# Seven block products for the first group of a channel mixer, and wider additions of key chunks

## The chip, the cores and the metric

One core of a Trainium2 chip. The metric is the time of one execution on the device in microseconds (us), lower is better; of several runs the median is given.

## The reference

Attention with capped scores (4 batches, 12 heads, 448 positions, head size 64), then a mixer over its output: a token product with a residual, and a channel product with a residual. All of it is in fp32.

```python
def _attn_ref(q, k, v, cap):
    scores = cap * np.tanh(scale * np.matmul(q, k.transpose(0, 1, 3, 2)) / cap)
    attn = np.exp(scores - np.max(scores, axis=-1, keepdims=True))
    attn = attn / (np.sum(attn, axis=-1, keepdims=True) + 1e-09)
    return np.matmul(attn, v)
...
def _moe_ref(x, w_tok1, w_tok2, w_ch1, w_ch2):       # x: (4, 448, 768)
    h = np.maximum(x.transpose(0, 2, 1) @ w_tok1, 0.0) @ w_tok2
    u = x + h.transpose(0, 2, 1)
    h2 = np.maximum(u @ w_ch1, 0.0) @ w_ch2          # 768 -> 1536 -> 768
    return u + h2
```

## The kernel before

**Precision.** Most products are made with three matmuls on two rounded parts of each operand: high x high, low x high, high x low (`TERMS`). So every operand of such a product needs a high part, a copy on ScalarE, and a low part, a subtraction of that copy on VectorE. The channel weights come as 64-bit numbers and are decoded in chunks of 512 columns (`decode`, lines 232 to 314): `first` on ScalarE, `second` and `third` on VectorE, then high and low parts. Two work tiles (`wz`) and two raw tiles (`wraw`) carry the chunks.

**Stages.** First the attention: for each pair of heads and each chunk of 128 keys (the last chunk, of 64 keys, is packed for two pairs of heads) TensorE makes scores (L424, L429, L435), ScalarE takes tanh and exp (L454, L462), TensorE multiplies by v (L502, L505). VectorE adds the exponentials over the key chunks in `acc` (`add_two` L524, `add_third` L531, `add_packed` L541: two instructions of 64x448 for each pair of heads), and TensorE sums `acc` over partitions (`add_rows`, L553). Beside it, in pieces, runs the token mixing of batches whose attention is done: transposes (L632), `tok1` (L660), `tok2` (L683).

Then the channel product, in 6 groups of 256 hidden columns. For a batch and a group, `ch1` makes 256 hidden columns from 768 (36 matmuls, L1033) and `ch2` adds their product with the second weights to `u`.

- In groups 1 to 5 the second product is done for two batches at once, `ch2_pair`: the hidden blocks of two batches and the weights are combined so that seven block products (p1 to p7) do the work of eight. That is 63 matmuls (7 products, 3 column blocks `mc`, 3 terms; L992) for 72. The operands are differences of hidden blocks, formed on GpSimd (`form`, L929), and each gets its high and low part (`split`, L953 and L958). Six operand tiles (`NO`) take them. Products run in two chains, a and b. A chain keeps adding to its PSUM banks, and after each product VectorE adds the banks to `u`: the first two banks of chain a by one wide instruction (L1020), the others singly (L1080). The chain's next product in the same bank waits for that addition (L984). The weights need seven blocks per chunk in place of four: `blocks` (L276, four sums on VectorE) and two high and two low parts (L289, L290, L298, L299).
- In group 0 it is done by batch, `ch2`: 36 matmuls (L1070), six additions (L1080), with high and low parts of all 256 hidden columns (L1048, L1051).

**The order.** The whole program's order is made when it is built. A planner (`Plan`, lines 106 to 185) holds a list of jobs for each engine, with an estimated cost, the estimated times of what they need, and a slack; among the jobs that are ready it takes the one with the lowest ready time plus slack. `plan.pe` is TensorE's planned time. `fill()` is called between matmul groups, and lays in up to 2500 ns of token mixing (`background`, `chunk`); where TensorE has to wait in the plan (`await_key`, `await_time`) it also takes such pieces, as long as there are any. `Ring`s count the buffers. Each engine then runs its own list in that order.

`first_group` (L1111) orders group 0: `ch1` of a batch if its split u is ready (at most two ahead of `ch2`), else a `ch2`, else a piece of token mixing. Batch 3 can be split only when all token mixing has ended, since its parts lie over the token weights (L1117 to L1120). The last `ch2` of the group comes after the first `ch1` of group 1. `open_m1` (L884) makes room for the operand tiles as soon as the attention has ended. The last pair of the kernel, (5, 1), has its own order of products (`FINISH`) and some low parts on GpSimd (`RELIEF`).

## Time and profile before

| | |
|---|---|
| median of 3 runs | 571.34 us (571.0 to 572.15) |
| the profiled execution | 571.16 us, of it span 569.4 us |
| granted TensorE clock | 0.998 |
| attention, with token mixing beside it | to about 194 us of the span |
| group 0, with the rest of the token mixing | about 189 to 294 us |
| groups 1 to 5 | about 294 to 569 us |

Times in the rows are microseconds of the span, unless marked ns. PE is TensorE's matmuls, PEld its weight loads, DVE VectorE, ACT ScalarE, POOL GpSimd; L12 is line 12 of the kernel. "a <- b" in brackets tells the idle time before an instruction and what ended it. The busy time of matmuls overlaps (367 ns each, though they start about every 204 ns), so the loads' starts are the better clock of TensorE.

### The profile page before, as it was taken

Reading aid. Unit: us, or ns where it says so; the run is one execution under the profiler, and the core shown is the slowest. Engines: PE = TensorE matmul, PEld = TensorE weight load, DVE = VectorE, ACT = ScalarE, POOL = GpSimd, SP = SyncE. Lnnn points to the kernel's source line nnn. Section 1 sums busy time; section 2 is a strip of 40 time slices with the busy share of each in tenths; the row PEclk is TensorE's granted clock in tenths of the full one; section 3 lists DMA queues with packets and bytes.
Section 4 is the critical chain, followed back from the end, with each engine's and each line's share of the span. In section 5 each row is a group of like instructions: output and inputs, shape, how many; then the busy total and the mean of one; then the engine's idle time right before and its main releaser. Section 6 shows DMA issues by size and latency. Waiting matters only on the chain.

```text
span 569.4 us, 8201 instructions
## 1 busy us (share of the span) xinstructions
PE 561.8 (99%) x3012; PEld 431.8 (76%) x3012; DVE 491.4 (86%) x857; ACT 298.9 (52%) x415; POOL 61.0 (11%) x66
## 2 busy tenths in 40 slices
PE   8999999999999999999999999999999999999996
PEld 2333455544646799999999899999999999998995
DVE  2999999998999998637859899988999899959597
ACT  7999999899899443222234433334342424224230
POOL 0000100000000000000004202020202030303050
PEclk9999999999999999999999999999999999999999
DMA  7554767666451232000212223112220212010055
GB/s 244 174 157 117 236 193 230 208 205 203 112 167 34 70 108 75 0 2 0 75 38 74 75 55 93 37 39 74 75 69 7 83 66 75 0 39 0 3 195 193
DMA packets 26780, 55.50 MB, mean 97 GB/s; under 512 B 7024, under 2 KB 16752, under 8 KB 26736
## 3 DMA queue, kind: packets, MB, share of 16 engines
q1 hardware_dynamic: 24144, 48.21, 26.7%
q0 software_dynamic: 2160, 6.39, 3.9%
q8 instruction: 24, 0.39, 0.3%
q10 hardware_dynamic: 432, 0.34, 0.2%
q14 instruction: 20, 0.16, 0.1%
HBM read 47.97 MB, written 5.59 MB: 94 GB/s over the span
## 4 chain that ended last, share of the span: by engine, by line
PE 85%; DVE 7%; ACT 3%; DMA 3%; issue 1%; SPq 0%; DVEq 0%; ACTq 0%
PE ps_g L1033 28%; PE ps_o L992 21%; PE ps_pv L502 7%; PE ps_qk L424 6%; PE ps_h L660 6%; PE ps_u L683 5%; PE ps_o L1070 5%; PE ps_t L632 2%; PE ps_s L553 2%; PE ps_qk L435 1%; PE ps_pv L505 1%; ACT e L454 1%; DMA wraw<-in_w 1%; DVE ops L958 1%; ACT e L462 1%
## 5 line engine op out<-in xcount | busy, mean ns | idle before, releaser
L1033 PE MATMUL ps_g<-uhl,wc 128*128 128x448 f32 x648 | 137.3, 367 | 0.0
L992 PE MATMUL ps_o<-ops,wc 128*128 128x448 f32 x630 | 131.0, 367 | 0.8 <-ACT hid L914 0.5
L1033 PEld LDWEIGHTS ps_g<-uhl,wc 128*128 128x128 f32 x648 | 120.9, 188 | 11.2 <-issue 0.7
L992 PEld LDWEIGHTS ps_o<-ops,wc 128*128 128x128 f32 x630 | 117.5, 188 | 13.0 <-issue 1.3
L1080 DVE TENSOR_TENSOR u<-u,ps_o 128x448 f32<-128x448 f32 (+1 forms) x163 | 92.3, 612 | 11.0 <-PE ps_o L1070 10.6
L953 ACT ACTIVATE ops<-hid 128x448 fp32r<-128x448 f32 x70 | 38.8, 574 | 116.4 <-POOL hid L929 70.3
L454 ACT ACTIVATE e<-ps_qk,tsc 128x896 f32<-128x896 f32 x84 | 81.6, 1037 | 7.9 <-PE ps_qk L424 4.0
L929 POOL TENSOR_TENSOR hid<-hid 128x448 f32<-128x448 f32 x40 | 48.5, 1212 | 345.9 <-ACT hid L914 287.3
L462 ACT ACTIVATE e<-e,near 128x896 f32<-128x896 f32 x84 | 85.5, 1077 | 0.1
L502 PE MATMUL ps_pv<-e,vn 128*64 128x448 f32 x288 | 60.5, 549 | 0.9 <-ACT e L462 0.9
L1020 DVE TENSOR_TENSOR u<-u,ps_o 128x896 f32<-128x896 f32 x36 | 38.9, 1081 | 16.9 <-PE ps_o L992 16.9
L958 DVE TENSOR_TENSOR ops<-hid,ops 128x448 fp32r<-128x448 f32 x67 | 45.4, 694 | 1.4 <-ACT ops L953 1.4
L1033 PE MATMUL ps_g<-last_u,wc 128*128 128x448 f32 x216 | 45.3, 367 | 0.0
L502 PEld LDWEIGHTS ps_pv<-e,vn 128*64 128x64 f32 x288 | 18.0, 136 | 34.7 <-issue 24.8
L1033 PEld LDWEIGHTS ps_g<-last_u,wc 128*128 128x128 f32 x216 | 40.6, 188 | 3.8
L255 ACT ACTIVATE wz<-wraw 128x512 f32<-128x512 f32 x36 | 23.8, 672 | 28.1 <-DVE wc L310 11.3
L660 PE MATMUL ps_h<-wc,last_u 128*128 128x384 f32 x176 | 33.3, 337 | 0.0
L683 PE MATMUL ps_u<-last_u,wc 128*128 128x448 f32 x144 | 32.8, 371 | 0.0
L660 PEld LDWEIGHTS ps_h<-wc,last_u 128*128 128x128 f32 x176 | 30.8, 188 | 1.8 <-issue 1.3
L683 PEld LDWEIGHTS ps_u<-last_u,wc 128*128 128x128 f32 x144 | 26.4, 188 | 6.0 <-issue 1.8
L1070 PE MATMUL ps_o<-ops,wc 128*128 128x448 f32 x144 | 30.9, 367 | 0.0
L541 DVE TENSOR_TENSOR acc<-acc,e 64x448 f32<-64x448 f32 x48 | 29.7, 619 | 1.3
(75 smaller groups left out, 632.7 us busy)
## 6 DMA issues: line engine op xcount, KB each, us to landing
wraw<-in_wc SPq DMA_DIRECT2D x36, 512.0 KB, 3.5
qkraw<-in_qk SPq DMA_DIRECT2D x23, 448.0 KB, 4.0
vn<-in_v SPq DMA_DIRECT2D x24, 224.0 KB, 3.3
rb<-rs SPq DMA_DIRECT2D x48, 112.0 KB, 3.3
out_t<-u SPq DMA_DIRECT2D x23, 224.0 KB, 2.0
qkhi<-in_qk POOLq DMA_DIRECT2D x12, 416.0 KB, 4.3
qkhi<-qkraw POOLq DMA_DIRECT2D x3, 416.0 KB, 3.9
wraw<-in_w SPq DMA_DIRECT2D x2, 512.0 KB, 6.0
```

Source lines behind the costliest of these rows:

```text
L454: nc.scalar.activation(e, ps[:, :, :S], AF.Tanh, scale=tsc)
L462: nc.scalar.activation(e, e, AF.Exp, scale=near)
L502: nc.tensor.matmul(o, vn[x % 3][:, j * NF + c], es[b, p, c][:, j], start=first, stop=last)
L660: nc.tensor.matmul(ps[:, :HALF], w, x, start=(n == 0), stop=(n == len(mm) - 1))
L683: nc.tensor.matmul(ps[:, :S], h1[:, hi, t, cs], w2s[:, wi, t, :], start=(n == 0), stop=(n == 3 * NT - 1))
L929: job(FORM, *cost, lambda: e.tensor_tensor(h[:, out], h[:, a], h[:, b], op=ALU.subtract), *deps, slack=500.0, key=("f", n, key))
L958: e.tensor_tensor(t[:, 1], src, t[:, 0], op=ALU.subtract)
L992: nc.tensor.matmul(ps[:, :S], wblock[mc][wi][:, a], x[:, xi], start=first and m == 0, stop=m == 2, skip_group_check=not first,)
L1020: nc.vector.tensor_tensor(u[b][:, cc:cc + 2], u[b][:, cc:cc + 2], ps[:, :, :S], op=ALU.add)
L1033: nc.tensor.matmul(ps[:, i, :S], w[:, wi, cc, fs], uhl[b][:, ui, cc, :], start=(n == 0), stop=(n == 3 * NC - 1))
L1070: nc.tensor.matmul(ps[:, :S], w[:, wi, i, cs], x[:, gi, i, :], start=(n == 0), stop=(n == 3 * GF - 1))
L1080: nc.vector.tensor_tensor(u[b][:, cc, r], u[b][:, cc, r], ps[:, r], op=ALU.add)
```

## The change

Group 0's second product is done by pairs, with seven products. Its weights are decoded with the seven blocks. The tile of group 0's second weights has room for the blocks of the first chunk and one more part, so those of the second and third chunk go into three of the six operand tiles, which group 0 doesn't use then: it has three for itself (`NI`, ring `oi`), and group 1's operands wait until group 0's second product is done. The two chunks in spare tiles wait for `m1`, the pool of the operand tiles. The chunk's sums take a tile of the attention's pool (`wi`, one buffer) until the later pool is open. The first pair is placed behind `ch1` of batch 1, the second behind the first `ch1` of group 1. Pair (0, 0) takes its products in the order `EARLY`: p1, p2, p7, p6, p4, p5, p3, and its chain b takes the other PSUM buffer of ring `a` for its first two banks, so that ring `c` stays with the token mixing. The splits of group 0 have a more urgent slack (`HASTE`).

The packed key chunks of two pairs of heads are added by one job with two instructions of 64x896 in place of two jobs with two of 64x448 each, once both pairs' sums exist.

In the last pair the low part of p3 goes to GpSimd too.

```diff
+NI = 3
+HASTE = -300.0
+EARLY = tuple(PRODUCTS[n] for n in (0, 5, 1, 2, 3, 4, 6))
-RELIEF = {(NG - 1, 1): ("p2", "p7", "p4")}
+RELIEF = {(NG - 1, 1): ("p2", "p7", "p4", "p3")}
...
+    def spot():
+        return "ws" if ("m2",) in done else "wi"
...
-                job("dve", 4 * 190, 4 * 190 + 70, blocks, (*key, 3), ("m2",), room("ws"), slack=slack, key=(*key, 5))
+                job("dve", 4 * 190, 4 * 190 + 70, blocks, (*key, 3), *([room("ws"), ("m2",)] if key[1] else [lambda: rings[spot()].room()]),
+                    slack=slack, key=(*key, 5))
...
-            s = held["s"] = late["m2"].tile([P, NS, P], F32, tag="ws", name="ws", bufs=2)
-            held["ws"] = rings["ws"].take(1)
+            at = spot()
+            s = held["s"] = (px if at == "wi" else late["m2"]).tile([P, NS, P], F32, tag=at, name=at, bufs=rings[at].n)
+            held["ws"] = rings[at].take(1)
...
+    def blocks_of(g, mc):
+        if g or mc == 0:
+            return wblock[mc]
+        spare = late["o"][:, NI:].rearrange("p n x s -> p n (x s)").rearrange("p n (k c) -> p n k c", c=P)
+        return (spare[:, 0], spare[:, 1]) if mc == 1 else (wend[0], spare[:, 2])
...
-                slack, since + mc * DU * st, after[1], wblock[mc] if combine else None,
+                slack, since + mc * DU * st, after[1] if g or mc == 0 else [("m1",)],
+                (lambda: blocks_of(g, mc)) if combine else None,
...
-        holds["e", b, p, c] = rings["e"].take(3 if c == NF else 2)
+        holds["e", b, p, c] = rings["e"].take(2)
...
             if i:
-                add_packed(b, p)
+                add_packed(b, p - 1)
...
-                keys = [(n, b, p - k) for n in ("third", "packed") for k in range(2)]
+                keys = [("third", b, p - 1), ("third", b, p), ("packed", b, p - 1)]
...
-        elif c == NF:
-            add_packed(b, p)
...
     def add_packed(b, p):
-        q, i = divmod(p, 2)
-
         def add():
-            for j in range(2):
-                r = half(i, j)
-                t = accs[b, q][0][r, i, j]
-                nc.vector.tensor_tensor(t, t, es[b, p - i, NF][r, i], op=ALU.add)
-            holds["e", b, p - i, NF].read(done["packed", b, p])
-
-        job("dve", 1272, 1260, add, ("add", b, p), ("exp", b, p - i, NF), slack=2500.0, key=("packed", b, p))
+            acc = accs[b, p // 2][0].rearrange("p i j s -> p (i j) s")
+            e = es[b, p, NF]
+            for r, t in ((slice(0, D), acc[:D, 0::3]), (slice(D, P), acc[D:, 1:3])):
+                nc.vector.tensor_tensor(t, t, e[r], op=ALU.add)
+            holds["e", b, p, NF].read(done["packed", b, p])
+
+        job("dve", 2030, 2150, add, ("add", b, p), ("add", b, p + 1), ("exp", b, p, NF), slack=2500.0, key=("packed", b, p))
...
-    w0, w0_steps = group_weights(0, slack=20000.0, since=65000.0, stagger=STAGGER)
+    w0, w0_steps = group_weights(0, combine=True, slack=WEIGHTS, since=SINCE, stagger=STAGGER)
...
+        done["m1",] = plan.pe
...
-        source = {"h0": ("r", n, 0), "h1": ("r", n, 0) if n[0] == NG - 1 else ("f", n, "t4"), "h3": ("f", n, "t2")}
+        source = {"h0": ("r", n, 0), "h1": ("r", n, 0) if n == (0, 0) or n[0] == NG - 1 else ("f", n, "t4"), "h3": ("f", n, "t2")}
...
-            deps = [source.get(of, ("f", n, of)), room("o")] + ([("sh", n, before)] if before else [])
+            deps = [source.get(of, ("f", n, of)), room("o" if n[0] else "oi")]
+            deps += [("sh", n, before)] if before else []
+            deps += [("ch2", 0)] if n[0] == 1 else []
...
-        return FINISH if n[0] == NG - 1 else PRODUCTS
+        return FINISH if n[0] == NG - 1 else EARLY if n == (0, 0) else PRODUCTS
...
-        job("act", 468, 568, high, *deps, slack=800.0, key=("sh", n, k))
+        job("act", 468, 568, high, *deps, slack=800.0 if n[0] else HASTE, key=("sh", n, k))
...
-            if mc == len(have):
+            if mc == len(have) and n == (0, 0):
+                tag = "a" if chain == "b" and mc == 0 else "b"
+                await_time(rings[tag].room)
+                if tag == "a":
+                    other = ps_a.tile([P, 2, 512], F32, tag="a", name="ps_o3")
+                    have += [other[:, 0], other[:, 1]]
+                    holds_of["b"] += [rings["a"].take(6)] * 2
+                else:
+                    have.append(ps_b.tile([P, 512], F32, tag="b", name="ps_o"))
+                    holds_of[chain].append(rings["b"].take(4 if chain == "a" else 3))
+            elif mc == len(have):
...
     def first_group(w):
-        started, g, at = 2, [], []
-        while len(g) < B:
+        started, n, pair = 2, 0, False
+        while n < B:
...
-            n, m = len(g), len(at)
-            t = plan.ready([("split", n, 0)]) if n < started and n - m < 2 else None
+            if n == 2 and not pair:
+                t = plan.ready([("s", (0, 0), PRODUCTS[0][0]), ("wc2", 0, 0)])
+            else:
+                t = plan.ready([("split", n, 0)]) if n < started else None
             if t is not None and t <= plan.pe + PATIENCE:
-                g.append(ch1(w[0], n))
-            elif m < n and (t := plan.ready([("g", 0, m)])) is not None and t <= plan.pe + PATIENCE:
-                ch2(w[1], m, g[m], False)
-                at.append(plan.pe)
+                if n == 2 and not pair:
+                    ch2_pair((0, 0), False)
+                    pair = True
+                else:
+                    ch1(w[0], n, 0, n // 2)
+                    n += 1
             elif not chunk():
                 rest()
             fill()
-        for m in range(len(at), B - 1):
-            ch2(w[1], m, g[m], False)
-        return w[1], B - 1, g[-1], False, 0
...
-            if g == 1 and b == 0:
-                ch2(*pend)
-                done["ch2", 0] = plan.pe
...
-            if b % 2:
+            if b % 2 or (g == 1 and b == 0):
                 if before is not None:
                     ch2_pair(before, False)
                     if before[1] == 1:
                         done["ch2", before[0]] = plan.pe
-                before = g, b // 2
+                before = (g, b // 2) if b % 2 else None
```

## Rows read from the trace of the kernel before

**Rows 1.** The page's first part: busy us, share of the span, instructions.

```profile
PE 561.8 (99%) x3012; PEld 431.8 (76%) x3012; DVE 491.4 (86%) x857; ACT 298.9 (52%) x415; POOL 61.0 (11%) x66
```

**Rows 2.** Weight loads' waits, 60 to 190 us: total us, times, longest.

```profile
PEld ps_pv L502 <- issue: 19.5, 76, 0.7
PEld ps_u L683 <- DVE acc L541: 0.7, 1, 0.7
```

**Rows 3.** Weight loads in order of time: start us, us, line, count.

```profile
194.43 0.16 PEld L553 LDWEIGHTS ps_s<-acc,ones 128*32 128x32 f32 x8 [0.31 <-ACT uhl L781]
...
221.91 2.33 PEld L1070 LDWEIGHTS ps_o<-ops,wc 128*128 128x128 f32 x12
...
259.81 12.25 PEld L1070 LDWEIGHTS ps_o<-ops,wc 128*128 128x128 f32 x60
...
344.74 12.87 PEld L992 LDWEIGHTS ps_o<-ops,wc 128*128 128x128 f32 x63
```

**Rows 4.** Order of time at the first pair of group 1.

```profile
317.25 2.92 PE L992 MATMUL ps_o<-ops,wc 128*128 128x448 f32 x13 [0.49 <-ACT hid L914]
...
318.77 1.09 DVE L1020 TENSOR_TENSOR u<-u,ps_o 128x896 f32<-128x896 f32 x1 [1.99 <-PE ps_o L992]
```

**Rows 5.** By stretch: busy us of PE, loads, VectorE, ScalarE, GpSimd; clock; DMA.

```profile
205.00:294.20 89.20, 89.20 (x464) 82.71 (x464) 60.27 (x112) 25.68 (x44) 0.00 (x0) 1.00 0.14 45
320.00:500.00 180.00, 180.00 (x882) 164.91 (x881) 168.11 (x303) 64.63 (x108) 33.14 (x28) 1.00 0.17 53
```

**Rows 6.** VectorE's groups: count, busy us, mean ns, idle before.

```profile
L1080 DVE TENSOR_TENSOR u<-u,ps_o 128x448 f32<-128x448 f32 x161 | 91.7, 615 | 11.0 <-PE ps_o L1070 10.6 <-PE ps_o L992 0.4
L1020 DVE TENSOR_TENSOR u<-u,ps_o 128x896 f32<-128x896 f32 x36 | 38.9, 1081 | 16.9 <-PE ps_o L992 16.9
L958 DVE TENSOR_TENSOR ops<-hid,ops 128x448 fp32r<-128x448 f32 x67 | 45.4, 694 | 1.4 <-ACT ops L953 1.4
L282 DVE TENSOR_TENSOR wz<-wz 128x128 f32<-128x128 f32 x15 | 4.4, 293 | 0.5
```

**Rows 7.** Group 0's weights, low parts: ns min/median/max, first and last start.

```profile
L310 DVE TENSOR_TENSOR wc<-wz,wc x6: 676/686/693, 115.9 to 210.5; 128x512 fp32r<-128x512 f32 x6
```

**Rows 8.** GpSimd's differences: ns min/median/max, first and last start.

```profile
L929 POOL TENSOR_TENSOR hid<-hid x40: 1142/1157/1537, 303.0 to 552.8; 128x448 f32<-128x448 f32 x40
```

**Rows 9.** Order of time at 303 us, GpSimd and VectorE.

```profile
303.00 4.39 POOL L929 TENSOR_TENSOR hid<-hid 128x448 f32<-128x448 f32 x3 [146.71 <-ACT hid L914]
...
303.47 1.35 DVE L310 TENSOR_TENSOR wc<-wz,wc 128x512 fp32r<-128x512 f32 x1 [0.22 <-ACT wc L306]
...
304.74 1.64 DVE L298 TENSOR_TENSOR wc<-wz,wc 128x512 fp32r<-128x512 f32 x1
...
306.31 1.51 DVE L299 TENSOR_TENSOR wc<-ws,wc 128x384 fp32r<-128x384 f32 x1
```

**Rows 10.** Weight loads of the token mixing, 221.3 to 260 us.

```profile
L683 PEld LDWEIGHTS ps_u<-last_u,wc 128*128 128x128 f32 x54 | 10.1, 188 | 0.8
L660 PEld LDWEIGHTS ps_h<-wc,last_u 128*128 128x128 f32 x45 | 8.0, 188 | 0.1
L632 PEld LDWEIGHTS ps_t<-ident,u 128*128 128x128 f32 x24 | 2.9, 140 | 0.3
```

**Rows 11.** High part of an operand on ScalarE, group.

```profile
L781 ACT ACTIVATE uhl<-u 128x448 fp32r<-128x448 f32 x18 | 9.7, 595 | 13.0 <-DVE u L689 13.0
```

**Rows 12.** Order of time in the tail: last pairs on TensorE, end of VectorE.

```profile
538.62 26.43 PE L992 MATMUL ps_o<-ops,wc 128*128 128x448 f32 x126
...
557.51 0.61 DVE L958 TENSOR_TENSOR ops<-hid,ops 128x448 fp32r<-128x448 f32 x1
...
559.05 7.18 DVE L1080 TENSOR_TENSOR u<-u,ps_o 128x448 f32<-128x448 f32 x14
```

**Rows 13.** Additions of key chunks: two of 64x448 in time, 128x896 as group.

```profile
191.19 1.25 DVE L541 TENSOR_TENSOR acc<-acc,e 64x448 f32<-64x448 f32 x2
...
L524 DVE TENSOR_TENSOR acc<-e 128x896 f32<-128x896 f32 x24 | 25.9, 1078 | 4.9 <-ACT e L462 4.8
```

More of the change, by code (lines that the diff above doesn't have):

```diff
@@ L949, in high @@
         def high():
[L950 to L952 removed]
+            ring = rings["o" if n[0] else "oi"]
+            t = late["o"][:, len(ring.holds) % ring.n]
+            operand[n, k] = t, ring.take(1)
             nc.scalar.activation(t[:, 0], src, AF.Copy)
```

24 lines of the change are left out of this document (13 added, 11 removed).

## The prediction

> **What bounds the kernel now.** I read the page's first part, then who waited for whom, then TensorE's weight loads in order of time, because the busy time of overlapping matmuls says little by itself. TensorE is busy 99% of the span, VectorE 86% [rows 1]. In the attention the loads' idle times never exceed 0.7 us apiece, and the same 0.7 stands where nothing was waited for at all ("issue"); the rows that name VectorE are single ones of that size, of which one is shown [rows 2]. So VectorE does not hold TensorE up there. Behind the attention the loads run end to end: 60 of the old channel product took 12.25 us, 0.204 us each, and a pair of 63 took 12.87 us [rows 3], also 0.204. One wait stands out in mid-kernel: the first pair of the second group began at 317 us after 0.49 us of idle matmul [rows 4]. From the attention's end on the kernel is bound by TensorE, so a matmul taken out there is worth 0.204 us, less what TensorE then waits.
>
> VectorE has room in the first group and little later: 60.3 of 89.2 us (68%) from 205 to 294 us, 168.1 of 180 us (93%) in the steady stretch, where TensorE still keeps the pace of rows 3 [rows 5].
>
> **The change, part by part.**
>
> *Matmuls.* Four batches of 36 become two pairs of 63: 144 less 126 is 18, at 0.204 us: **-3.67 us**, all of it in the bound engine.
>
> *VectorE and GpSimd in the first group.* Out go 24 additions of 0.615 us (14.8 us) and four low parts of 896 columns (4.3 us at the wide addition's price). In come, for a pair, four wide additions of 1.081 and thirteen of 0.615 us, so 24.6 us for two pairs, and 14 low parts of 448 columns, 8.6 us at 0.615 each (their mean, 0.694, has blocked ones in it) [rows 6]. Each of three weight chunks gains four block sums of 0.292 us [rows 6] and a second, narrower low part of at most the 0.686 us of the first [rows 7]: 1.7 to 1.9 us, three times, 5.4 us. The sum is +19.5 us: 60.3 becomes 79.8 us in a stretch that shrinks to about 85.5, or 93%. That is the steady stretch's share, so by itself it costs TensorE nothing. ScalarE has 25.7 us of work there [rows 5]; fourteen high parts of 0.60 us (the price of rows 11) add 8, which it can take. GpSimd gets eight differences of 1.157 us, the median [rows 8], in time that it now spends idle.
>
> Those eight are not free for VectorE. Where three of them ran at 303 us, in 4.39 us, three VectorE subtractions of two SBUF tiles beside them took 1.35, 1.64 and 1.51 us [rows 9] in place of 0.69 and less: some 0.8 us more each. Over the whole kernel it is far less: 67 low parts at 0.694 against 0.615 us lose 5.3 us to 40 differences, 0.13 us each [rows 6, 8]. The ends are 8 x 0.13 = 1 us and 8 x 0.8 = 6.4 us of VectorE; I take the lower, since it averages the same pattern, and the upper makes a rival. The Trainium skill ("SBUF — State Buffer", "Who interferes with whom") says that a VectorE instruction with two SBUF inputs and a GpSimd instruction that reads SBUF shut each other out for a whole instruction; the trace at 303 us agrees, and were all eight to block so, the sum would come out near 573 us instead.
>
> *What covers the waits.* From 221 us, where the old product begins, to 259.8 us, where its last 60 matmuls run unbroken [rows 3], TensorE also has 22 us of token mixing: 54 and 45 matmuls and 24 transposes [rows 10]. Those 60 matmuls then hide the splits of the last batch. After the change the token pieces must lie between the products of one pair of 63. By the code it offers 17 places with up to 2.5 us each, but chains of transpose, product and eviction keep the pieces from coming faster than they do now. So I expect the token work to end near the pair's end, and one of two bills comes. If it ends earlier, the last two products of the new order, p5 and p3, meet in the same bank: the wide addition starts 0.30 us after its sixth matmul's slot (317.25 plus 6 x 0.204, to 318.77 us) [rows 4] and takes 1.08 us, three matmuls cover 0.61 us, so TensorE waits **0.8 us**; and the third batch's first product takes the bank pair just used, **0.8 us** again. If it ends later, splitting the last batch starts only after the third batch's product: 0.60 us on ScalarE [rows 11], 0.62 on VectorE and two handovers, 1.3 to 1.5 us uncovered. I take **+1.6 us**; bounds 0 (pieces left for every wait) and 3.5 (a loaded VectorE doubles each wait).
>
> *Weights.* The last of the six low parts of group 0's weights starts at 210.5 us [rows 7], about 11 us before the pair. The second-product chunks now take their sums in one spare tile, so the three follow each other. Two also wait for their place in the spare operands, free once the attention's last row sums ran at 194.4 us [rows 3]; that is over before they need it. Queued behind a waiting chunk are only the next one and, by the two work tiles, the second group's first ones. I cost it at nothing: token pieces fill a start that is late by some us. If that cover is gone, 2 us.
>
> *Second pair, first pair of group 1.* The second pair has three operand tiles, so four of its seven splits fall inside its own 12.87 us. 12.3 us of additions and 2.5 of splits make 14.8 us of busy VectorE; back to back such instructions start 0.51 us apart, 14 in 7.18 us [rows 12], which makes it about 13. It just fits. What it pushes back is the second group's weights, and these stand before the pair that already waits at 317 us. I take **+0.3 us**, between -0.5 (that wait gone) and +3.
>
> *Attention.* Two additions of 64x448 take 1.25 us together; twelve times, four of them (2.5 us) give way to two of 64x896, 2.15 us at the price of 128x896 [rows 13]: 4 to 5 us less of VectorE. As rows 2 show no wait of TensorE that this would shorten, I cost it at **0**; the order of pieces shifts, so -1.2 to +0.7.
>
> *Tail.* The split at 557.5 us leaves VectorE, which from there runs without a break to 566.2 us, while TensorE ends at 565.05 us [rows 12]. The end comes forward by at most that 0.61 us and not past the eviction of TensorE's own last matmul: **-0.3 us**, between 0 and -0.5. GpSimd has until the last product for it, some 5 us.
>
> **Sum.** The profiled execution took 571.16 us: 569.4 us of span and 1.76 us around it; it stands 0.18 us below the median of the runs, 571.34. 571.16 - 3.67 + 1.6 + 0.3 - 0.3 = 569.1 us; the median would be 569.3. Between them: **569.2 us**.
>
> **Rivals.**
> - *All of it arrives.* Token pieces stay for every wait in the first pair, and group 1 starts as now: 571.2 - 3.7 - 0.3 + 0.3 = 567.5 us. For it: 17 places, more than the pieces need if each were ready. Against: the last token product follows an eviction of over 1 us with nothing else to lay in.
> - *The gain is given back.* The second pair and the weights of group 1 make the wait at 317 us 2 us longer: 571.1 us. For it: it is the place where TensorE waits already, behind weight decoding and splits. Against: three batches of first products, 22 us, stand between the second pair and that one.
> - *Slower.* VectorE becomes the bound of the first group: GpSimd's differences block its subtractions at the rate of rows 9, and 6.4 us on top of 79.8 make 86.2 us in 85.5. As operands come only three ahead, it cannot even that out. It decides where blocked time exceeds about 5.7 us; from there each us more is one that TensorE waits, and the uncovered waits of the pairs are at their upper bounds (3.5 + 2). With 5.5 us of waits it is 573.0 us. For it: the rows at 303 us. Against: the steady stretch bears four differences a pair at 93%.
> - *The change does not do what it says.* If a late third chunk holds the first pair back until the token work is used up, its products stand without cover: 571 us, counted with the second rival.
>
> **How the numbers follow.** A difference under 0.2%, 1.14 us, can't be told from none here: faster ends at 570.2, slower begins at 572.5 us. Forecast (568.2 to 570.1): 0.42. All of it: 0.22. Given back: 0.20. Slower: 0.16. So faster 0.64, same 0.20, slower 0.16. The range takes in the first three, at the low end with the wait at 317 us gone: 567.0 to 572.2; the fourth stays out. The forecast's own range is 568.2 to 570.1.
>
> **What would show it.** Right: 756 matmuls on the pair's line and none of the old product; VectorE's busy time up by some 15 us over the kernel; one or two idle times of 0.5 to 1.5 us on the weight loads between 235 and 275 us, naming a wide addition or a split; the first pair of group 1 waiting under 1.5 us. The attention should end where it did, within 1 us. The first rival shows no such idle time; the second a first pair of group 1 that waits 2 us or more; the third idle times in both pairs, VectorE above 97% and many subtractions of 1.3 us and more. Wrong altogether would be an attention that became clearly shorter or longer: then VectorE did set its pace.

## The result, and the profile after

The changed kernel is slower: 575.53 us (median of 5 runs, 574.81 to 576.76) against 571.88 us (571.0 to 572.87) for the kernel before on the same chip, a ratio of 1.006 with an interval of 1.0045 to 1.0075. The profiled execution took 575.02 us, 573.2 of it span: 3.8 us more span than before. The forecast was 569.2 us.

First the page's parts 1 and 4 of the changed kernel, the first of which answers to [rows 1], and part 4 of the kernel before.

```profile
PE 560.2 (98%) x2994; PEld 428.0 (75%) x2994; DVE 507.0 (88%) x867; ACT 307.3 (54%) x432; POOL 71.7 (13%) x75
...
PE 68%; DVE 21%; ACT 4%; DMA 3%; issue 3%; SPq 1%; DVEq 0%; ACTq 0%
...
PE 85%; DVE 7%; ACT 3%; DMA 3%; issue 1%; SPq 0%; DVEq 0%; ACTq 0%
```

The 18 matmuls are gone (3012 to 2994) and VectorE has the 15.6 us more that were forecast, so the change does what it says. But the chain that ended last now runs through VectorE for 21% of the span; before it was 7%, and TensorE 85%.

Three points in time show where the 3.8 us arose: the start of the first `ch1`, the start of the first pair of group 1, and the end. The first `ch1` begins at 188.48 us (before at 188.90, where 0.86 us of transposes lay ahead of it that now come behind it). **The stage from there to group 1's first pair takes 132.78 us where it took 128.34.** From that pair to the end it is 251.94 against 252.16. So all of the loss lies in group 0, the stage that lost 18 matmuls. Its weight loads, in order of time, with the waits that stand out (before had only the last of them, 0.87 us, and one of 0.7 us that both have):

```profile
210.14 0.42 PEld L647 LDWEIGHTS ps_t<-ident,u 128*128 128x128 f32 x4 [0.47 <-DVE wc L684]
...
218.00 2.36 PEld L698 LDWEIGHTS ps_u<-last_u,wc 128*128 128x128 f32 x12 [1.24 <-ACT ops L971]
...
229.37 0.51 PEld L1020 LDWEIGHTS ps_o<-ops,wc 128*128 128x128 f32 x3 [0.63 <-ACT wc L654]
...
267.80 6.78 PEld L1061 LDWEIGHTS ps_g<-last_u,wc 128*128 128x128 f32 x34 [1.22 <-DVE last_u L799]
...
287.36 0.50 PEld L1020 LDWEIGHTS ps_o<-ops,wc 128*128 128x128 f32 x3 [1.75 <-ACT ops L971]
...
291.55 0.51 PEld L1020 LDWEIGHTS ps_o<-ops,wc 128*128 128x128 f32 x3 [0.64 <-issue]
...
295.75 0.51 PEld L1020 LDWEIGHTS ps_o<-ops,wc 128*128 128x128 f32 x3 [0.65 <-issue]
...
321.26 8.88 PEld L1020 LDWEIGHTS ps_o<-ops,wc 128*128 128x128 f32 x44 [1.64 <-ACT hid L930]
```

With three more before 216 us (0.47, 0.52, 0.31) there are five groups: (a) 3.0 us between 200 and 222 us, (b) 0.63 in the first pair, (c) 1.22 at the splits of the last batch, (d) 3.04 in the second pair, (e) 1.64 before group 1's first pair, 0.77 more than before. That is 8.7 us; what has to be explained is the stage's 4.44 us more, plus the 3.67 us that the 18 matmuls should have saved, less the 0.86 us of transposes that moved into it: 7.25 us. The idle time of a load overstates the pause of the matmuls by some tenths.

The row of a load names what came last for the load; the row of the matmul names what the product itself waited for. For the longest wait of (a) and of (d) that is VectorE (L658 makes a low part of a transposed token piece), and ScalarE's `hid`, which (e) waits for, had waited for VectorE's last low parts:

```profile
218.03 2.71 PE L698 MATMUL ps_u<-last_u,wc 128*128 128x448 f32 x12 [0.89 <-DVE wc L658]
...
287.39 0.84 PE L1020 MATMUL ps_o<-ops,wc 128*128 128x448 f32 x3 [1.41 <-DVE u L1048]
...
320.29 0.92 ACT L930 ACTIVATE hid<-ps_g 128x896 f32<-128x896 f32 x1 [1.04 <-DVE ops L976]
```

The chain that ended last, in order of time over the last part of the stage, leaves TensorE at the end of the token work and comes back to it only at group 1's first pair; in between it runs through VectorE, but for two instructions on ScalarE at 271.07 and 320.29 us (in the kernel before, the same chain stays on TensorE up to 302 us):

```profile
262.91 3.66 PE ps_u L698 x18
...
266.59 0.62 DVE u L704
...
320.29 0.93 ACT hid L930
...
321.26 0.88 PE ps_o L1020 x3
```

Now who was full. Busy time by stretch of the changed kernel (columns: stretch, its length, then PE, loads, VectorE, ScalarE, GpSimd, clock, DMA):

```profile
188.50:222.00 33.50, 32.24 (x172) 27.66 (x171) 32.04 (x65) 15.67 (x28) 3.53 (x3) 1.00 0.26 80
222.00:267.00 45.00, 44.68 (x239) 41.43 (x237) 30.44 (x56) 14.21 (x26) 1.15 (x1) 1.00 0.00 1
267.00:321.20 54.20, 50.19 (x241) 44.86 (x241) 52.89 (x89) 22.02 (x37) 10.60 (x8) 1.00 0.22 67
```

and the stretches of the kernel before that answer to them:

```profile
188.90:222.00 33.10, 33.10 (x184) 29.97 (x182) 31.32 (x60) 14.51 (x26) 0.00 (x0) 1.00 0.26 86
222.00:260.00 38.00, 38.00 (x204) 35.63 (x203) 20.62 (x38) 10.66 (x20) 0.00 (x0) 1.00 0.01 4
260.00:317.20 57.20, 56.76 (x277) 51.59 (x275) 45.41 (x82) 18.56 (x31) 5.78 (x4) 1.00 0.21 61
```

VectorE over the whole stage is at 115.4 of 132.7 us, 87%, which looks harmless. By stretch it is 96%, 68% and **97.6%**. In the middle it idles nearly 15 us while TensorE works on token mixing and the third batch; then, when the token work ends at 266.2 us, the last batch's splits, the second group's weights and the second pair's operands and additions come free together. In the kernel before the same last stretch was at 79%.

A full stretch alone does not make TensorE wait, though. In the kernel before VectorE is as full for 25 us of the steady stretch, and TensorE's loads run there without a wait; and the kernel of e1 below, which has lost most of these waits, is at 98% too (before, then e1):

```profile
345.00:370.00 25.00, 25.00 (x124) 22.90 (x123) 24.69 (x47) 8.89 (x15) 4.87 (x4) 1.00 0.19 59
...
267.00:318.00 51.00, 49.80 (x242) 45.06 (x241) 50.00 (x81) 21.72 (x37) 11.00 (x8) 1.00 0.21 66
```

What counts is what VectorE has to do ahead of the instruction that TensorE needs next.

That is read in VectorE's own queue, in order of time, ahead of the wide addition at 286.17 us (L1048 is before's L1020):

```profile
276.81 4.05 POOL L945 TENSOR_TENSOR hid<-hid 128x448 f32<-128x448 f32 x3 [47.52 <-ACT hid L930]
...
277.18 1.25 DVE L291 TENSOR_TENSOR ws<-wz 128x128 f32<-128x128 f32 x1
278.46 1.20 DVE L292 TENSOR_TENSOR wz<-wz 128x128 f32<-128x128 f32 x1
279.58 0.28 DVE L293 TENSOR_TENSOR ws<-ws,wz 128x128 f32<-128x128 f32 x1
279.89 1.13 DVE L294 TENSOR_TENSOR ws<-wz,ws 128x128 f32<-128x128 f32 x1
...
283.72 0.62 DVE L976 TENSOR_TENSOR ops<-hid,ops 128x448 fp32r<-128x448 f32 x1
284.26 0.29 DVE L291 TENSOR_TENSOR ws<-wz 128x128 f32<-128x128 f32 x1
284.58 1.14 DVE L292 TENSOR_TENSOR wz<-wz 128x128 f32<-128x128 f32 x1
285.64 0.28 DVE L293 TENSOR_TENSOR ws<-ws,wz 128x128 f32<-128x128 f32 x1
285.95 0.29 DVE L294 TENSOR_TENSOR ws<-wz,ws 128x128 f32<-128x128 f32 x1
286.17 1.08 DVE L1048 TENSOR_TENSOR u<-u,ps_o 128x896 f32<-128x896 f32 x1
```

The pair began at 281.95 us, so by the spacing of [rows 4] its first wide addition could have started at about 283.5 us (281.95 + 6 x 0.204 + 0.30). It started 2.7 us later, behind group 1's decoding, and TensorE's next product in those banks began right behind its end (287.25). Part of the backlog is the lock: block sums that take 0.28 us took 1.13 to 1.25 us while GpSimd formed the differences, the pattern of [rows 9]. The Trainium skill ("SBUF — State Buffer", "Who interferes with whom") says that a VectorE instruction with two SBUF inputs contends with a GpSimd instruction that reads SBUF, and the trace agrees: these sums have both inputs in SBUF. From 287.16 us on the pair cannot catch up: two products take TensorE 18 x 0.204 = 3.67 us and come 4.19 us apart (287.36, 291.55, 295.75), the time in which VectorE does one wide and four single additions and two low parts without a gap.

The tail, in order of time:

```profile
565.84 2.21 DVE L1108 TENSOR_TENSOR u<-u,ps_o 128x448 f32<-128x448 f32 x4
568.46 1.75 DVE L1108 TENSOR_TENSOR u<-u,ps_o 128x448 f32<-128x448 f32 x4 [0.40 <-PE ps_o L1020]
```

VectorE waits for TensorE there, where it ran without a break before [rows 12]: from group 1's first pair to the end 0.2 us are gained, and no more was to be had from the moved split.

### The profile page after: what moved, and what is told of

Same layout as the page of the kernel before. It is cut to its first block, busy times and chain, and to the rows that moved or that the text cites. A ratio compares the mean times of both kernels' runs of the same rounds, so it can differ in the third digit from the quotient of the medians.

```text
span 573.2 us, 8220 instructions
## 1 busy us (share of the span) xinstructions
PE 560.2 (98%) x2994; PEld 428.0 (75%) x2994; DVE 507.0 (88%) x867; ACT 307.3 (54%) x432; POOL 71.7 (13%) x75
## 4 chain that ended last, share of the span: by engine, by line
PE 68%; DVE 21%; ACT 4%; DMA 3%; issue 3%; SPq 1%; DVEq 0%; ACTq 0%
PE ps_o L1020 23%; PE ps_g L1061 22%; PE ps_pv L519 5%; PE ps_qk L443 4%; PE ps_h L675 4%; PE ps_u L698 4%; ACT e L473 2%; DVE u L1108 2%; DVE ops L976 2%; DVE wz L277 1%; ACT e L481 1%; DVE wz L276 1%; DVE acc L548 1%; DVE u L1048 1%; PE ps_qk L454 1%
## 5 line engine op out<-in xcount | busy, mean ns | idle before, releaser
L1020 PE MATMUL ps_o<-ops,wc 128*128 128x448 f32 x700 | 151.8, 368 | 3.9 <-DVE u L1048 2.2
L1020 PEld LDWEIGHTS ps_o<-ops,wc 128*128 128x128 f32 x700 | 130.2, 188 | 18.2 <-ACT ops L971 2.2
L971 ACT ACTIVATE ops<-hid 128x448 fp32r<-128x448 f32 x84 | 46.5, 574 | 126.5 <-POOL hid L945 73.2
L945 POOL TENSOR_TENSOR hid<-hid 128x448 f32<-128x448 f32 x48 | 58.0, 1209 | 341.7 <-ACT hid L930 249.8
L1108 DVE TENSOR_TENSOR u<-u,ps_o 128x448 f32<-128x448 f32 x165 | 93.1, 613 | 1.1 <-PE ps_o L1020 0.9
L1048 DVE TENSOR_TENSOR u<-u,ps_o 128x896 f32<-128x896 f32 x44 | 47.6, 1082 | 16.8 <-PE ps_o L1020 16.8
L976 DVE TENSOR_TENSOR ops<-hid,ops 128x448 fp32r<-128x448 f32 x80 | 54.8, 700 | 1.4 <-ACT ops L971 1.4
L930 ACT ACTIVATE hid<-ps_g 128x896 f32<-128x896 f32 x24 | 22.1, 919 | 19.4 <-PE ps_g L1061 13.7
L541 DVE TENSOR_TENSOR acc<-e 128x896 f32<-128x896 f32 x24 | 26.0, 1082 | 5.5 <-ACT e L481 5.4
```

Source lines behind the costliest of these rows:

```text
L945: job(FORM, *cost, lambda: e.tensor_tensor(h[:, out], h[:, a], h[:, b], op=ALU.subtract), *deps, slack=500.0, key=("f", n, key))
L971: nc.scalar.activation(t[:, 0], src, AF.Copy)
L976: e.tensor_tensor(t[:, 1], src, t[:, 0], op=ALU.subtract)
L1020: nc.tensor.matmul(ps[:, :S], blocks_of(g, mc)[wi][:, a], x[:, xi], start=first and m == 0, stop=m == 2, skip_group_check=not first,)
L1048: nc.vector.tensor_tensor(u[b][:, cc:cc + 2], u[b][:, cc:cc + 2], ps[:, :, :S], op=ALU.add)
L1108: nc.vector.tensor_tensor(u[b][:, cc, r], u[b][:, cc, r], ps[:, r], op=ALU.add)
```

## The experiments

"Stage" is the time from the first `ch1` to the first pair of group 1, in the profiled execution: 128.34 us before, 132.78 us changed. Ratios are to the kernel before on the same chip, with their interval. The first `ch1` is not at the same place in the work everywhere: in e10 to e13, as in the kernel before, the 0.86 us of transposes lie ahead of it, and in e14 11 loads of token mixing (1.97 us) come behind it that lie ahead of it elsewhere. In e1, e3 and e9 instructions are left out after the order is planned, so everything else keeps its place; in the other runs the planner lays out the whole program anew, so other pieces move too.

| run | us | before | ratio | stage |
|---|---|---|---|---|
| e1_light | 571.33 | 572.07 | 0.9978 (0.9966 to 0.999) | 128.39 |
| e2_slack | 574.68 | 572.07 | 1.0046 (1.0029 to 1.0064) | 131.37 |
| e3_noform | 573.36 | 572.07 | 1.0022 (1.0009 to 1.0034) | 129.98 |
| e4_packed_relief | 572.59 | 572.07 | 1.0009 (0.9994 to 1.0023) | 129.75 |
| e5_since | 578.9 | 572.33 | 1.0147 (1.0102 to 1.0191) | 136.46 |
| e6_form_dve | 575.14 | 572.33 | 1.0054 (1.0034 to 1.0073) | 131.68 |
| e7_since_form | 574.26 | 572.33 | 1.0042 (1.0028 to 1.0056) | 131.12 |
| e8_since_form_slack | 573.54 | 572.33 | 1.002 (1.0007 to 1.0034) | 129.97 |
| e9_light_noform | 570.84 | 572.02 | 0.9977 (0.9966 to 0.9988) | 128.11 |
| e10_old_packed | 582.56 | 572.02 | 1.0182 (1.0161 to 1.0203) | 138.55 |
| e11_light_noform_old | 575.69 | 572.02 | 1.0052 (1.0034 to 1.0071) | 131.60 |
| e12_all_old | 577.57 | 572.02 | 1.0089 (1.007 to 1.0108) | 134.27 |
| e13_form_old | 577.03 | 572.21 | 1.0081 (1.0062 to 1.01) | 134.93 |
| e14_late | 575.47 | 572.21 | 1.0062 (1.0046 to 1.0077) | 135.97 |

### Is VectorE too full, or only in the wrong order?

**e1_light**: 5.1 us of VectorE taken out of group 1's decoding (limits and shifts left out), nothing else moved.

```diff
-            nc.vector.tensor_scalar(zf, zf, 2.0 ** -31, 2.0 - 2.0 ** -23, op0=ALU.max, op1=ALU.min)
-            nc.vector.tensor_scalar(z, z, 4, 1, op0=ALU.logical_shift_left, op1=ALU.logical_shift_right)
+            if key[0] != ("wc1", 1) and key[:2] != ("wc2", 1):
+                nc.vector.tensor_scalar(zf, zf, 2.0 ** -31, 2.0 - 2.0 ** -23, op0=ALU.max, op1=ALU.min)
+                nc.vector.tensor_scalar(z, z, 4, 1, op0=ALU.logical_shift_left, op1=ALU.logical_shift_right)
```

> The changed kernel, with the two range-and-shift instructions of VectorE (0.85 us a chunk, six chunks, 5.1 us) left out of group 1's weight decoding, in the same order of work; group 1's weights are then not the right ones. Theory 'full' (VectorE has more work between 267 and 321 us than time, 52.9 of 54.2 us busy, so every late addition, split and weight there is late for that): the waits of the weight loads there, 1.2 + 1.8 + 0.6 + 0.6 + 1.6 us, shrink by 3 to 5 us in all, and the time is 3 to 5 us below the changed kernel's 575.5 us. Theory 'order' (only the places in VectorE's queue are wrong: weight decoding stands ahead of the wide addition at 286 us): one chunk's 0.85 us stands ahead of that addition, so about 1 us. Theory 'tiles' (three operand tiles starve the second pair): no change, within 0.5 us.

As the theory 'full' has it: the time fell by 4.2 us, and the stage by 4.4 us, to 128.39. Of the waits, (d) went from 3.04 to 0.43 and (a) from 3.0 to 0.75; (c) stayed at 1.22 to the hundredth, (e) came to 1.34. 4.4 us for 5.1 us of VectorE: in the two full stretches, in this order of work, almost each us on VectorE is one on TensorE. The theories 'order' (about 1 us) and 'tiles' (no change) missed.

**e2_slack**: the same work, group 1's weights less urgent for the planner.

```diff
-                g + 1, ([("tok",)] if g == 0 else (), [("ch2", g)]), combine=True, slack=60000.0
+                g + 1, ([("tok",)] if g == 0 else (), [("ch2", g)]), combine=True, slack=60000.0 if g else 120000.0
```

> The changed kernel with one constant changed: group 1's weight jobs get a slack of 120 us for 60, so that the planner puts the second pair's splits and additions and the last batch's splits ahead of them; no work is added or taken away. 'Order': the three waits in the second pair (1.75, 0.64, 0.65 us) go and nothing comes in their place: 3 us below 575.5. 'Full': the waits of the second pair shrink, but the weights come later and the first pair of group 1, which waits 1.6 us now, waits 2 to 4 us: between 1 us faster and 1 us slower than 575.5. 'Tiles': no change in the second pair.

The second pair's waits are unchanged (1.74, 0.64, 0.65); only (e) fell, from 1.64 to 0.24, where 'full' expected it to grow. But the edit didn't test the order in the pair: VectorE's queue ahead of the wide addition, at 285.96 us here, holds the same instructions in the same order as in the changed kernel. It differs only from 305 us on, and there the other order was worth 1.4 us of (e). So whether another order of the same work would spare the pair its waits stays open. There may be room for it: VectorE also decodes three chunks of group 2's weights between 302 and 321 us, which TensorE needs from 334 us on.

### Is it GpSimd's lock?

**e3_noform**: the four differences of pair (0, 1) are left out, the order is the same.

```diff
-            job(FORM, *cost, lambda: e.tensor_tensor(h[:, out], h[:, a], h[:, b], op=ALU.subtract),
+            job(FORM, *cost, lambda: None if n == (0, 1) else e.tensor_tensor(h[:, out], h[:, a], h[:, b], op=ALU.subtract),
```

> The changed kernel without the four GpSimd differences of pair (0, 1), in the same order of work; its products then take undifferenced blocks. Theory 'lock' (GpSimd's differences block VectorE's two-input instructions: between 276 and 286 us four sums of 0.29 us took 1.25, 1.20, 1.13 and 1.14 us, 3.6 us more): those four return to 0.29 us and the waits of the second pair fall by 2 to 3.6 us, most of it in the 1.75 us wait. 'Full' agrees with that, since 3.6 us leave the full stretch, and expects 2 to 3.5 us. 'Order' without the lock expects under 1 us, 'tiles' none.

The waits in the second pair went from 3.04 to 0.22 us and the stage fell by 2.8 us; (c) and (e) stayed. 'Lock' and 'full' both expected this. Weight loads in order of time:

```profile
269.89 6.79 PEld L1061 LDWEIGHTS ps_g<-last_u,wc 128*128 128x128 f32 x34 [1.22 <-DVE last_u L799]
...
295.25 0.51 PEld L1020 LDWEIGHTS ps_o<-ops,wc 128*128 128x128 f32 x3 [0.22 <-issue]
...
320.77 4.39 PEld L1020 LDWEIGHTS ps_o<-ops,wc 128*128 128x128 f32 x22 [1.64 <-ACT hid L930]
```

The pair's own work on VectorE is the same as above. Started without a backlog, it is covered.

**e6_form_dve**: group 0's eight differences on VectorE, so that nothing locks and VectorE has eight instructions more.

```diff
-            e, cost = (nc.gpsimd, (1170, 1250)) if FORM == "gps" else (nc.vector, (536, 620))
-            job(FORM, *cost, ...
+            on = FORM if n[0] else "dve"
+            e, cost = (nc.gpsimd, (1170, 1250)) if on == "gps" else (nc.vector, (536, 620))
+            job(on, *cost, ...
```

> The changed kernel with the eight differences of group 0 on VectorE (0.62 us) in place of GpSimd (1.16 us). 'Lock': the four sums that took 1.13 to 1.25 us between 277 and 286 us take 0.29 again, -3.6 us, against +2.2 us for four more instructions: the waits of the second pair fall from 3.0 to 1.5 to 2 us; the first pair's two blocked low parts (1.24 and 1.33 us) too, against +2.2 us. In all 0.5 to 2 us below 575.5. 'Full' without the lock (only the amount of VectorE's own work counts): 4.4 us more work, 1 to 3 us slower.

Of the second pair's waits the 1.75 us went and 0.63 and 0.64 stayed; three small waits came in the first pair (0.19, 0.26 and 0.41 us). The time is 0.4 us below the changed kernel's 575.53 and inside its runs: just short of what 'lock' expected, while 'full' without the lock, 1 to 3 us slower, is out. What the lock takes, the work itself takes nearly as well. The 1.24 us of (a) stayed as they were, so they are not the lock's.

**e9_light_noform**: e1 and e3 together.

> The changed kernel without the limits and shifts of group 1's weights (5.1 us of VectorE) and without the four differences of pair (0, 1); both are left out of the computation. Theory 'VectorE is overfull from 267 to 321 us': the waits of the second pair end below 0.4 us in sum, the wait before the first pair of group 1 falls below 1.3 us, and what is left of the bills is the 1.22 us at the splits of the last batch, about 0.75 us before the first pair and the new wait near 140 us; with 3.67 and 0.2 us gained that is 570.0 to 571.0 us where the kernel before takes 572.1, 0.5 us or less below the kernel with the lighter decoding alone, since the two edits remove the same waits. Rival 'the lock between GpSimd and VectorE is a cost of its own, beside the fullness': the two gains add, 2.2 us below the kernel with the lighter decoding alone, 569.1 us.

The two do not add, as the theory has it: 128.11 us of stage after 128.39 with e1 alone, 570.84 us. Only (e), 1.45 us, stayed above the 1.3 us that was expected. The pair's waits are nearly gone:

```profile
267.20 6.79 PEld L1062 LDWEIGHTS ps_g<-last_u,wc 128*128 128x128 f32 x34 [1.22 <-DVE last_u L800]
...
292.57 0.50 PEld L1021 LDWEIGHTS ps_o<-ops,wc 128*128 128x128 f32 x3 [0.22 <-issue]
...
317.77 12.36 PEld L1021 LDWEIGHTS ps_o<-ops,wc 128*128 128x128 f32 x61 [1.45 <-ACT hid L931]
```

So lock and decoding are two loads on one queue, not two causes.

### Can the load be moved into the idle stretch?

**e5_since**: group 1's weights enter the plan 55 us later, to be decoded in VectorE's idle time from 251 us on.

```diff
-                g + 1, ([("tok",)] if g == 0 else (), [("ch2", g)]), combine=True, slack=60000.0
+                g + 1, ([("tok",)] if g == 0 else (), [("ch2", g)]), combine=True, slack=60000.0, since=0.0 if g else plan.pe + 55000.0
```

> The changed kernel with group 1's weight jobs held back by 55 us of planned time, so that the first two chunks' decoding (4.4 us of VectorE at 209 to 217 us, where VectorE has no idle time) moves to about 250 us, where VectorE idles 9 us in 15; same work otherwise. Theory 'uneven' (VectorE is full only in parts, and the loss ahead of the first pair comes from work that could wait): the waits of the weight loads between 209 and 218 us (0.47, 0.52, 0.31, 1.24 us) fall by about 2 us, those from 267 us on stay: 2.0 to 2.6 us below 575.5. Theory 'sums' (what fills VectorE there are group 0's own seven blocks, 5 us of new work): the waits stay, under 0.7 us gained.

Both theories missed: 3.4 us above the changed kernel. Two chunks did go there (their decoding ran from 252.1 to 257.8 us) and the 1.24 us of (a) is gone. But with two work tiles no more than two chunks can wait for the token weights' place; fewer token pieces fell into the first pair (70 loads of token mixing against 81 in the changed kernel), TensorE waited 0.5 to 1.1 us six times there, and the third chunk of group 1's first weights came behind block sums that GpSimd had locked: 3.52 us at 281.8 us.

**e7_since_form** (e5 and e6 together) and **e8_since_form_slack** (with e2's slack too):

> Both of the last two edits. If the two losses are separate, ahead of the first pair and in the second, the gains add: 2.5 to 4.5 us below 575.5, about 572. If they are one backlog that only moves, no better than the better of the two.

> The two edits and the slack of 120 us, which had brought the first pair of group 1 forward (its wait fell from 1.64 to 0.24 us). If the three losses are separate: about 571, as the kernel before, within 1 us. If the backlog of VectorE only moves: no better than the run with two edits.

They come to 574.26 and 573.54 us, each between what its two theories expected. Each edit takes away the waits that it aims at (the 3.52 us of e5 in e7; (e) to 0.24 in e8) and leaves others. The best of them is still slower than the kernel before. More operand tiles, so that the second pair's splits lie ahead of it as in the later groups, were not tried.

### What are the other two parts of the change worth?

**e4_packed_relief**: the kernel before, with the wide packed additions and the moved split of p3 alone.

```diff
-RELIEF = {(NG - 1, 1): ("p2", "p7", "p4")}
+RELIEF = {(NG - 1, 1): ("p2", "p7", "p4", "p3")}
...
-                t = accs[b, q][0][r, i, j]
-                nc.vector.tensor_tensor(t, t, es[b, p - i, NF][r, i], op=ALU.add)
+            for r, t in ((slice(0, D), acc[:D, 0::3]), (slice(D, P), acc[D:, 1:3])):
+                nc.vector.tensor_tensor(t, t, e[r], op=ALU.add)
```

> The kernel before with only the two small parts of the change: packed key chunks added by two 64x896 instructions, and p3's low part of the last pair on GpSimd. By the prediction's steps: attention within 0.5 us of before, the tail 0 to 0.5 us shorter, so -0.3 us of 571.9 (within 0.2%). If the packed additions are what costs the changed kernel its time (a 2 us block on VectorE ahead of urgent work), this is slower by 1 us or more, with the attention ending later.

No difference that can be measured. In the tail VectorE waits for TensorE as in the changed kernel. A new wait of TensorE stands at 140 us, and VectorE's queue shows why (its rows, and one weight load):

```profile
136.36 0.24 DVE L590 RECIPROCAL sums<-sums 128x14 f32<-128x14 f32 x1 [1.75 <-DMA sums<-xs]
...
139.24 1.02 DVE L392 TENSOR_TENSOR qklo<-qkraw,qkhi 128x832 fp32r<-128x832 f32 x1
...
140.31 0.19 PEld L424 LDWEIGHTS ps_qk<-qkhi,qklo 64*128 64x128 f32 x2 [1.37 <-DVE qklo L392]
```

A reciprocal of 0.24 us waited 1.75 us for its DMA with the whole queue behind it, the low part of q and k among it, which TensorE needed. Every kernel with the wide additions but the last below (e14) has such a wait of TensorE there, 0.8 to 2.4 us (in e3, with 2.40, the instruction that waits for a DMA is the addition just ahead of the reciprocal); in the kernel before, the reciprocal stood later in the list and waited for nothing.

**e10_old_packed**: the changed kernel with the additions of before.

> The changed kernel with the packed key chunks added as before, by two instructions of 64x448 for each pair of heads. Theory 'the wide packed additions cost a wait of TensorE near 140 us, behind a reciprocal that waits for its DMA': that wait is gone and the time is 0.5 to 1.5 us below the changed kernel, 574.0 to 575.0 us where the kernel before takes 572.1. Rival 'the packed additions relieve VectorE in the attention by some 4 us': the attention becomes longer without them, 575.5 us or more.

582.56 us, 7 us more than with the wide additions. The theory is refuted, and the rival has the sign but not the reason: the wait at 140 us is gone and the attention is no longer than in the kernel before (first `ch1` at 188.67 us), but group 0's seven-block weights are late. With the wide additions one chunk was finished before 190 us and the last at 211 us; without them none before 190 us and the last at 218 us. The three differences then fell into the first pair itself:

```profile
222.19 4.55 POOL L949 TENSOR_TENSOR hid<-hid 128x448 f32<-128x448 f32 x3 [66.13 <-DVE wc L688]
...
222.56 1.64 DVE L276 SCALAR_TENSOR_TENSOR wz<-wraw,wz 128x512 int32<-128x512 int32 x1
224.23 1.52 DVE L277 SCALAR_TENSOR_TENSOR wz<-wraw,wz 128x512 int32<-128x512 int32 x1
225.68 1.54 DVE L980 TENSOR_TENSOR ops<-hid,ops 128x448 fp32r<-128x448 f32 x1
...
227.27 0.19 PEld L1024 LDWEIGHTS ps_o<-ops,wc 128*128 128x128 f32 x1 [2.60 <-DVE ops L980]
```

That is not all of the 7 us. Four more waits stand in the pair (1.09, 0.92, 0.51 and 0.70 us), with only 60 loads of token mixing inside it, and the longest wait of e10 comes later: 3.50 us at 284.35 us, for group 1's third chunk, as in e5. e5 and e14 have the same four waits (within 0.02 us) with the wide additions in, e5 with group 0's weights as early as in the changed kernel; so these are not the late weights'.

**e11_light_noform_old** and **e12_all_old**: the additions of before in e9 and in e8.

> The two parts left out as in the experiment before last (limits and shifts of group 1's weights, differences of pair (0, 1)), and the packed key chunks added as before. Theory: the bills that are left are 1.22 us at the splits of the last batch and 0.75 us before the first pair, so 569.5 to 570.3 us where the kernel before takes 572.1: the forecast's 2 us, once VectorE is given the room that the forecast assumed. Rival 'the wait near 140 us is a matter of order, not of the packed additions': no difference from the kernel with the wide packed additions, within 0.3 us.

> The whole computation: the changed kernel with group 1's weights from 55 us later and with a longer slack, group 0's differences on VectorE, and the packed key chunks added as before. Theory: 0.5 to 1.5 us below the same kernel with the wide packed additions (573.5 us), so 572.0 to 573.0 us, level with the kernel before (572.1 us) and not better, since the second group of work still asks more of VectorE from 267 to 321 us than the kernel before did. Rival: with the queue's order mended the 3.67 us arrive after all, 570.5 us or less.

575.69 and 577.57 us, 4.9 and 4.0 us more than with the wide additions: both theories and both rivals missed. Waits of this kind stand in the first pair (1.16, 1.42, 1.09 and 0.93 us in e11), and e12 has 2.99 us before group 1's third chunk.

**e13_form_old** (e10 with e6's edit) and **e14_late** (the changed kernel, group 0's weights loaded later in the plan):

```diff
-SINCE = 65000.0
+SINCE = 95000.0
```

> The changed kernel with the packed key chunks added as before and group 0's eight differences on VectorE in place of GpSimd. Without the wide packed additions the changed kernel took 582.6 us, 7 us more than with them. Theory 'the late weights push the three differences of the first pair into the pair itself, where they block two subtractions and the operand that TensorE waits for': without GpSimd's differences the wait of 2.60 us in the first pair and the half clock behind it go, 577.0 to 579.0 us. Rival 'the late weights themselves leave the first pair too few token pieces, whatever makes the differences': 581.5 us or more.

> The changed kernel, wide packed additions kept, with group 0's channel weights loaded from 95 us instead of 65 us in the plan. Theory 'what the wide packed additions are worth is room for the first seven-block chunk before 190 us': with the chunk late all the same, the attention is as long as in the changed kernel and the first pair waits as without the wide additions: 579 us or more where the changed kernel takes 575.5. Rival 'the additions' own time counts, not the weights' place': 575.0 to 576.5 us.

e13 came to 577.03 us, in its theory's range: without GpSimd's burst the wait of 2.60 us is gone, and by the medians 5.5 of e10's 7 us with it. In its profiled execution, the slowest of its six, 1.89 and 1.60 us stand in the first pair in its place, and 2.66 us before group 1's third chunk, with no lock.

e14 has the rival's time, but not by a shorter attention. The last chunk was as late as in e10 (217 us). The first `ch1` began 2.1 us earlier (186.37 us) because 11 loads of token mixing (1.97 us) now come behind it, and they account for 2 of the 3.2 us by which the stage is longer. So the late weights, with all that the plan moved beside them, cost 1 us in the profiled execution and nothing that the medians show. What e10 lost is thus neither one wait nor the late weights by themselves; by its waits it is the lock and the decoding inside the pair, too few token pieces for it and the late third chunk together, with the half clock of the last section behind two of the waits. How much of it is VectorE's room and how much is the order that the planner lays anew is not settled.

## Why the prediction was wrong

- **Matmuls, right.** 18 fewer; with VectorE relieved by work that is left out (e9) the stage is shorter, and that kernel 0.23% faster (0.12% to 0.34%) than before.
- **VectorE's load, right in size, wrong in what it means. This is the step that failed.** The forecast of some 15 us more was met (15.6), in part by luck: 4.9 us of it is blocked time where 1 was forecast. The step was "That is the steady stretch's share, so by itself it costs TensorE nothing". It spread 79.8 us evenly over 85.5 and costed the load by its share. The runs show in its place that VectorE's queue holds TensorE up: behind the token work it had 52.9 of 54.2 us to do, the chain that ended last runs through it there, and 5.1 us taken out of it gave back 4.4 us (e1). Batch 3's splits and group 1's weights wait for the token weights' place, so that work came at once, behind 14.6 us of idle time. Why the steady stretch bears the same share without a wait is not shown; it has six operand tiles to work ahead with, where the second pair has three, and more tiles were not tried.
- **Second pair and first pair of group 1, +0.3 forecast, 3.8 measured** ((d) 3.04 and 0.77 more at (e)), above even the bound of 3. "It just fits" counted only the pair's own instructions. They fit if VectorE has no backlog when the pair begins (e3: 0.22 us); its first wide addition began 2.7 us late.
- **The lock, taken at its lower end, 1 us.** Six instructions beside group 0's differences took 1.13 to 1.33 us in place of 0.29 and 0.62, 4.9 us more together, and e3 shows that the second pair's share was worth 2.8 us of TensorE. The upper end, 6.4 us, was the nearer. I had taken the mean over the kernel for the price, though [rows 9] showed the like place at its full price. Beside weight decoding and low parts the differences lock; an addition from PSUM at 217.92 us, beside a difference, took its 0.62.
- **Waits at the first pair, +1.6 forecast.** The bill for splitting the last batch came, at 1.22 us (1.3 to 1.5 forecast). The one for the shared bank did not. In its place came 3.0 us before the pair (a) and 0.63 within, which no step had. VectorE's share there rose only from 95 to 96%, but group 1's decoding now stood among the token pieces' copies; without part of that decoding (e1) 2.25 of the 3.0 us went. The lock has no part in it: the two locked low parts, at 218.46 and 220.15 us, come behind the last of these waits.
- **Weights, costed at nothing.** In the changed kernel they were in time (211 us), and e14, with 217 us, lost at most 1 us by it. But in time they were only with the wide packed additions, which I had treated as a part of its own.
- **Attention, 0.** Right for that part alone (e4), wrong as a term of the sum: parts that load one engine don't add. Inside the change, taking it back cost 7 us (e10). The reading that loads never idle above 0.7 us holds from 60 us on; at 10.15 us one stands at 1.63, which no term uses.
- **Tail, -0.3.** -0.2 measured, cut off by TensorE's own last matmul as said.

The rival "slower" named the mechanism, VectorE as the bound of group 0, and one of its sources, the blocked subtractions. It was priced at 573.0 us because it too counted from the average over the whole group: it let VectorE bind only beyond 5.7 us of blocked time. Against the last stretch alone there was no such reserve: 1.3 us of idle time were left in it.

## What to carry to other kernels

Before an edit is called free because an engine has room, divide its busy time at the points where work comes free (a buffer's release, a stage's end): 87% over this stage was 68% and 97.6%. Then look at each full piece for what another engine needs next and what stands ahead of that in the queue; the steady stretch was as full and cost nothing, so the share only says where to look. The Trainium skill ("Perfetto Trace Analysis", "Identifying the Most-Contended Engine") takes the engine with the highest occupancy as the most contended, and judges TensorE's headroom by its share of peak work or by its weight loads' busy share; by the loads VectorE (86%) stood ahead of TensorE (76%) before the change [rows 1]. That agrees with what the change ran into, but not with the kernel before, where the chain that ended last ran through TensorE for 85% of the span. And test the parts of a change together as well as alone: one that was worth nothing by itself cost 7 us when it was taken out of the whole.

## What was not expected of the hardware

An instruction with one tensor input was held up by GpSimd too: a shift on VectorE took 1.25 us beside a difference on GpSimd at 315 us, where it takes 0.43. The Trainium skill (the same section of "SBUF — State Buffer") lists `tensor_scalar`, which this shift is, among the operations that can take the shared ports under some conditions on their operands, and the row agrees.

In e10 the wait of 2.60 us cost more than itself. By stretch:

```profile
222.00:227.00 5.00, 3.06 (x17) 2.38 (x15) 4.97 (x5) 2.04 (x5) 4.39 (x3) 1.00 0.27 93
227.00:229.00 2.00, 1.72 (x7) 1.40 (x8) 2.00 (x4) 0.17 (x1) 0.00 (x0) 0.71 0.71 242
229.00:231.00 2.00, 2.00 (x7) 1.68 (x6) 1.92 (x5) 0.90 (x2) 0.00 (x0) 0.50 0.00 0
231.00:233.00 2.00, 1.29 (x8) 0.90 (x6) 0.97 (x3) 0.60 (x1) 0.00 (x0) 0.93 0.03 8
```

TensorE stood idle up to 227.3 us; then the granted clock fell to 0.50, the 1.2 GHz level, and a matmul's load took 0.33 us in place of 0.19 until about 231 us. The profiled executions show the same fall in other places: in e10 once more (0.50 from 286 to 289 us) behind the 3.50 us, in e5, e12 and e13 behind 3.52, 2.99 and 2.66 us, and in the attention of e3 and e1 behind waits of 2.40 and 1.77 us near 140 us. None of the changed kernel's own waits, 1.75 us at most, did that in its profiled execution (0.999 over its span), nor did the 1.89 us of e13. So the length of one wait doesn't settle it.
